# New planner costs and new order for a fused linear-attention and softmax-attention kernel

## The chip, the cores and the metric

One core of a Trainium2 chip. The metric is device time in microseconds of one execution, median over runs. The engines are TensorE (PE; its weight loads are PEld), VectorE (DVE), ScalarE (ACT), GpSimd (POOL) and SyncE (SP, whose queue issues most DMAs).

## The reference

Two attention blocks over 2048 tokens of width 512, 32 heads of 16, each with its own input and weights; their outputs are set side by side.

```python
# A: linear attention
phi = lambda t: jnp.where(t > 0, t + 1, jnp.exp(t)) + 1e-6
pq, pk = phi(q), phi(k)
kv = jnp.einsum("bhsd,bhse->bhde", pk, v)
z = jnp.einsum("bhsd->bhd", pk)
num = jnp.einsum("bhqd,bhde->bhqe", pq, kv)
den = jnp.einsum("bhqd,bhd->bhq", pq, z)[..., None] + 1e-6
o_a = num / den                      # then @ wo
# B: softmax attention
scores = jnp.einsum("bhqd,bhkd->bhqk", q, k) * Dh ** -0.5
p = softmax(scores)
o_b = jnp.einsum("bhqk,bhkd->bhqd", p, v)   # then @ wo
```

## The kernel before

Nearly all work is B's scores: 32 heads x 2048 x 2048. They are cut in 2048 blocks of 128 keys by 512 queries. A unit is four heads (row groups g of TensorE) with one chunk of 512 queries, 64 blocks; there are 32 units. Each block has one matmul for its scores (`qk`, L899) and is then exponentiated by one of two ways.

- **ScalarE's way.** The scores stand in the five PSUM banks `pS`; one ACTIVATE (L1111) reads two banks (1024 columns) or three (1536) and writes `PT` in f16. One output matmul for each block (L1306, PT with VV) adds it to `pPV`. Two slots of `pS` alternate, so that TensorE fills one while ScalarE reads the other.
- **VectorE's way.** The scores stand in one of two banks `pD`, or in the third bank of `pS` when ScalarE does not need it. One TENSOR_SCALAR (L1015) makes of them the integer whose bits are an f16 exponential, in `DI`. Two shifted copies of it follow, made from groups of up to two blocks (`DG`): most on GpSimd (L1226 for one group or several in one instruction, L1201 for a first and a second copy of two groups together), some on VectorE (L1170, and L1235 for the last unit alone). Three output matmuls take the three versions (one with the weights VX, two with VV), whose sum is a better exponential.

VectorE also evicts every projection (L595, L638, L647, L709, L764), normalises units (L1335, L1340, L1346), and does the second half of A's phi (L722, L724), whose exponential is ScalarE's EA (L721). A's jobs and the projections (`bjobs`, `ajobs`) are laid between the scores.

The order of the work is not written by hand. When the program is built, a planner keeps a clock `T` for each engine and again and again takes the piece of work that could start first; what it takes is added to its engine's queue. Engines then run their queues strictly in that order and wait on semaphores, so the planner's numbers set only the order. They are

- durations: an exponential is a fixed part + 0.000833 us a column (in `fill_act_cand`'s `run` and in `phi_stages`), a projection round `MM`, a round of output matmuls 0.218 us (`pv_cand`);
- delays between engines: `LTO` from the engine that writes to the one that reads, `LPE` from an engine's end until what it read can be filled again, `SWT` when TensorE changes the kind of matmul;
- the table `SEG`: one row of knobs for each 12 us of TensorE's planned time. `RW` is how early a score matmul may stand before ScalarE needs it, `RMX` and `DPR` how many blocks go to VectorE with it and how soon, `DBL` and `PBL` the backlog of VectorE and GpSimd above which no further block goes that way, `PVR`, `PVQ` and `PVO` how output matmuls are gathered, `DE2` and `DE3` from how few remaining blocks of the last unit on no block goes to VectorE and shifts of the last unit are VectorE's. `NZ` and `SD` add a noise, with its seed, to ties.

The last unit ends in `last_unit` (L1396 to L1401, two halves), four output projections (L1358) and four stores.

Of the kernel before, what the change touches and what calls it, by code (L numbers as in the profile page):

```python
# [238 lines left out]
def bass_concat_heads__linear_attn_block__softmax_full_mha__prompt_kernel(nc, A_x, A_wqkv, A_wo, B_x, B_wqkv, B_wo, out):  # L239
# [11 lines left out]
    JM = 2  # L251
    JX = 1
# [76 lines left out]
    )  # L329
    GB = 0.0  # L330
    PM = -0.025
    JN = 4
    KSL = 0.02
    PFX = 0.272
    FIDLE = 0.8
    AEND = 60.0
    RW = 0.3
    EQ = 20.0
    FPB = 4.0
# [28 lines left out]
    with es:  # L368
# [675 lines left out]
        def fill_act_cand():  # L1044
# [24 lines left out]
            def run(st, en):  # L1069
# [34 lines left out]
                if tk:  # L1104
                    d_emit(tk, T["pe"])
                w = 512 * len(bl)
                d = 0.052 + w * 0.000833
                exps.append(d)
                def ex(st_, en_):
                    exps.pop(0)  # L1110
# [626 lines left out]
```

## Time and profile before

| | |
|---|---|
| median of 3 runs | 661.06 us (660.82 to 661.22) |
| the profiled execution | 660.68 us, span 657.8 us |
| TensorE's granted clock | 1.000 |
| busy share PE, DVE, ACT, POOL | 97%, 97%, 98%, 90% |
| instructions of DVE, ACT, POOL | 1099, 696, 407 |

The span goes from the first to the last instruction; some 2.9 us of the execution's time lie around it. Busy time counts a record from its start to its end. Records of one engine can overlap, so two engines can both look full; how far apart records end tells more.

### The profile page before, as it was taken

To read this page: it belongs to the slowest core of one execution; us is meant where nothing else is said; L and a number is where in the kernel's file an instruction comes from. 1 tells how busy PE (TensorE), PEld (TensorE's weight loads), DVE (VectorE), ACT (ScalarE), POOL (GpSimd) and SP (SyncE) were. 2 spreads that over 40 slices of the span, in tenths; PEclk is the share of its full clock that TensorE was granted. 3 is DMA by queue.
4 is the path that set the end of the run, shared out by engine and by line. 5 is a ranking of instruction groups with operands and counts; after the bars stand their busy time and mean duration, and the time that the engine had idled before them with its cause. 6 is when DMAs were issued, how large, how long until landed. Compare 5 with 4: busy or idle time off the path is not lost.

```text
span 657.8 us, 19264 instructions
## 1 busy us (share of the span) xinstructions
PE 640.0 (97%) x8318; PEld 214.3 (33%) x8318; DVE 635.1 (97%) x1099; ACT 643.1 (98%) x696; POOL 589.9 (90%) x407
## 2 busy tenths in 40 slices
PE   8999999999999999999999999999999999999996
PEld 5333333232333333332232232322223322232222
DVE  4999999999999999999999999999999999999995
ACT  6999999999999999999999999999999999999995
POOL 5899999999999999999999999999999989999892
PEclk9999999999999999999999999999999999999999
DMA  9701010110101111002111011100110010011001
GB/s 185 202 1 33 3 34 2 33 26 10 34 2 34 34 34 35 1 17 74 26 33 42 1 34 34 26 11 8 23 25 13 2 33 26 9 34 49 22 29 46
DMA packets 53227, 21.75 MB, mean 33 GB/s; under 512 B 44176, under 2 KB 52624, under 8 KB 53136
## 3 DMA queue, kind: packets, MB, share of 16 engines
q1 hardware_dynamic: 51664, 19.80, 12.9%
q8 instruction: 67, 1.10, 0.7%
q10 hardware_dynamic: 1472, 0.66, 0.4%
q14 instruction: 24, 0.20, 0.1%
HBM read 4.46 MB, written 4.19 MB: 13 GB/s over the span
## 4 chain that ended last, share of the span: by engine, by line
ACT 84%; PE 11%; DVE 3%; DMA 1%; issue 0%; DVEq 0%
ACT PT L1111 82%; PE pPV L1306 4%; PE pS L899 3%; PE pD L609 2%; ACT EA L721 2%; DVE DI L1015 2%; DMA xTb<-in_B_x_dram 1%; DMA KNa<-VNa 1%; PE pD L899 1%; PE pS L609 0%; PE pD L1358 0%; DVE DI L1235 0%; PE pS L1442 0%; PE pS L1358 0%; DVE VNa L811 0%
## 5 line engine op out<-in xcount | busy, mean ns | idle before, releaser
L1111 ACT ACTIVATE PT<-pS 128x1024 f16<-128x1024 f32 (+1 forms) x658 | 630.7, 1151 | 1.7 <-PE pS L899 1.0
L1226 POOL TENSOR_SCALAR DI<-DI 128x2048 int16<-128x2048 int16 (+2 forms) x289 | 481.0, 1664 | 41.0 <-DVE DI L1015 22.9
L1015 DVE TENSOR_SCALAR DI<-pD 128x512 int16<-128x512 f32 x475 | 312.7, 679 | 6.0 <-PE pD L899 2.2
L899 PE MATMUL pS<-QT,KM 32*128 32x512 bf16 x1573 | 260.5, 384 | 7.4 <-ACT PT L1111 6.0
L1306 PE MATMUL pPV<-PT,VV 128*17 128x512 f16 x1361 | 235.3, 381 | 0.2 <-DVE OT L1335 0.2
L1306 PE MATMUL pPV<-DI,VV 128*17 128x512 f16 x1374 | 229.9, 382 | 0.3 <-POOL DI L1226 0.2
L899 PE MATMUL pD<-QT,KM 32*128 32x512 bf16 x475 | 171.2, 384 | 0.6 <-DVE DI L1015 0.6
L1306 PE MATMUL pPV<-DI,VX 128*17 128x512 f16 x687 | 160.5, 381 | 0.3 <-DVE OT L1335 0.2
L899 PEld LDWEIGHTS pS<-QT,KM 32*128 32x128 bf16 x1573 | 65.2, 91 | 243.2 <-ACT PT L1111 197.2
L1015 DVE TENSOR_SCALAR DI<-pS 128x512 int16<-128x512 f32 x212 | 143.8, 678 | 0.2 <-PE pS L899 0.2
L1170 DVE TENSOR_SCALAR DI<-DI 128x1056 int16<-128x1056 int16 x109 | 74.1, 687 | 0.5
L1201 POOL TENSOR_SCALAR DI<-DI 128x2048 int16<-128x2048 int16 x37 | 70.2, 1897 | 4.7 <-POOL DI L1226 1.6
L1306 PEld LDWEIGHTS pPV<-DI,VV 128*17 128x17 bf16 x1374 | 51.0, 88 | 46.9 <-issue 34.1
L1306 PEld LDWEIGHTS pPV<-PT,VV 128*17 128x17 bf16 x1361 | 52.4, 88 | 41.0 <-issue 31.3
L1306 PEld LDWEIGHTS pPV<-DI,VX 128*17 128x17 bf16 x687 | 36.4, 88 | 21.2 <-issue 15.4
L899 PEld LDWEIGHTS pD<-QT,KM 32*128 32x128 bf16 x475 | 40.6, 91 | 7.1 <-DVE DI L1015 3.6
L609 PE MATMUL pD<-xTb,Wb 128*32 128x512 bf16 x368 | 29.2, 384 | 0.6 <-DVE VV L709 0.5
L609 PE MATMUL pD<-Wa,xTa 128*32 128x256 bf16 x704 | 28.8, 275 | 0.1
L1335 DVE STREAM_TRANSPOSE OT<-pPV 128x512 f32<-128x512 f32 x31 | 21.9, 707 | 0.1
L1341 POOL TENSOR_TENSOR OT<-OT,ZR 128x256 bf16<-128x256 f32 x31 | 19.2, 620 | 3.0 <-DVE ZR L1340 1.4
L609 PE MATMUL pD<-Wa,KNa 128*32 128x512 bf16 x240 | 19.6, 384 | 0.8 <-DMA KNa<-VNa 0.7
L609 PEld LDWEIGHTS pD<-Wa,xTa 128*32 128x32 bf16 x704 | 15.2, 96 | 11.0 <-issue 6.6
(144 smaller groups left out, 381.1 us busy)
## 6 DMA issues: line engine op xcount, KB each, us to landing
out_dram<-KNa SPq DMA_DIRECT2D x31, 128.0 KB, 1.7
Wa<-in_A_wqkv_dram SPq DMA_DIRECT2D x1, 1536.0 KB, 8.6
KM<-KR SPq DMA_DIRECT2D x96, 16.0 KB, 1.8
Wb<-in_B_wqkv_dram SPq DMA_DIRECT2D x2, 384.0 KB, 4.1
Wb<-in_B_wqkv_dram SPq DMA_DIRECT2D x1, 512.0 KB, 4.7
Wa<-in_A_wo_dram SPq DMA_DIRECT2D x1, 512.0 KB, 5.5
Wa<-in_B_wo_dram SPq DMA_DIRECT2D x1, 512.0 KB, 3.7
ON<-in_B_x_dram ACTq DMA_DIRECT2D x1, 256.0 KB, 3.1
```

Of the source, the lines that this page charges most:

```text
L609: ins = self.e.matmul(out_[32 * g:32 * g + 32], lhsT=lhsT[:, 32 * g:32 * g + 32], rhs=rhs, start=start, stop=stop, tile_position=(0, 32 * g))
L721: ("act", 0.052 + n * 0.000833, f_ev("act", lambda e, bk: e.activation(EA[:, 0:n], f32v(bk)[:, c0:c0 + n], ACTF.Exp), [], ["EA"])),
L899: return e.matmul(dst, lhsT=KM[32 * g:32 * g + 32, Gp % 2, e_, j * 128:(j + 1) * 128], rhs=QT[32 * g:32 * g + 32, Gp % 2, c * 512:(c + 1) ...
L1015: sch.add("dve", lambda e: e.tensor_scalar(DI[:, di_at(0, buf) + i * 512:di_at(0, buf) + (i + n) * 512], f32v(DBANK[b0], n * 512), ESC, EB ...
L1111: sch.add("act", lambda e: e.activation(PTf[:, p0 * 512:p0 * 512 + w], S5[:, c0:c0 + w], ACTF.Exp, scale=SC), reads=skeys(sl, len(bl)), wr ...
L1170: sch.add("dve", lambda e: e.tensor_scalar(gapped(DI, di_at(v, buf), wide // 32, 32), DI[:, di_at(0, buf) - 32:di_at(0, buf) + w], 1.0, fl ...
L1201: sch.add("pool", lambda e: e.tensor_scalar(dv, sv, 1.0, float(SHIFT[0]), op0=ALU.mult, op1=ALU.add), reads=keys, writes=[("DI", v_, x) fo ...
L1226: sch.add("pool", lambda e: e.tensor_scalar(dv, sv, 1.0, sh_, op0=ALU.mult, op1=ALU.add), reads=keys, writes=[("DI", v, x) for x in best])
L1306: sch.add("pe", lambda e, g=g, j=j, c0=c0, V_=V_, r2=r2, P=P, first=first, last_=last_: e.matmul(PVb[32 * g:32 * g + 17, 0:512] if len(P.s ...
L1335: sch.add("dve", lambda e: e.transpose(OT[:, 0, :], PVb[:, 0:512]), reads=[("PV", g) for g in range(4)], writes=[("OT", 0)])
L1341: ("pool", 0.69, f_op("pool", lambda e: e.tensor_tensor(xn[:, :, 16 * e_:16 * e_ + 16], o[:, :, 0:16], zr.unsqueeze(2).broadcast_to([128, ...
```

## The change

It changes numbers of the planner, and so the order on every engine; no instruction's kind is new. The fixed part of an exponential rises from 0.052 to 0.0635 us and now stands for the distance between the ends of two ACTIVATEs in a row; the delay from TensorE to VectorE rises from 0.2 to 0.243; smaller corrections go with them. All 54 rows of `SEG` are new. Each has two more knobs that were constants before: `PTW`, by which two evictions from pD may become one, and `JN`, how many groups one shift may take. No pair of evictions is joined in the order that results.

```diff
     SEG = (
-        (0.0,0.1,4,3.0,6,1,6,4,9.0,26,3.0,7.0,0.8,0.8,2,7.0,2.0,2.5,0.5,2,1,0.3,4,10,0,0),
...
+        (0.0,0.2,4,0.8,6,1,8,2,10.0,28,2.5,6.0,0.5,2.5,2,4.0,2.0,2.5,0.5,2,1,0.1,8,0,-9.0,4,2,6),
...
-        LPE = {"dve": 0.136, "act": 0.176, "pool": PM, "pe": 0.2, "dma": 0.12}
-        LTO = {("pe", "dve"): 0.2, ("pe", "act"): 0.215, ("act", "dve"): 0.155, ("dve", "pool"): 0.163, ("pool", "dve"): 0.07, ("dve", "act"): 0.15}
-        SWT = 0.106
+        LPE = {"dve": 0.139, "act": 0.16, "pool": PM, "pe": 0.243, "dma": 0.12}
+        LTO = {("pe", "dve"): 0.243, ("pe", "act"): 0.215, ("act", "dve"): 0.137, ("dve", "pool"): 0.166, ("pool", "dve"): -0.03, ("dve", "act"): 0.15}
+        SWT = 0.107
...
-        MM = 0.218
+        MM = 0.224
...
-                ("act", 0.052 + n * 0.000833, f_ev("act", lambda e, bk: e.activation(EA[:, 0:n], f32v(bk)[:, c0:c0 + n], ACTF.Exp), [], ["EA"])),
+                ("act", 0.0635 + n * 0.000833, f_ev("act", lambda e, bk: e.activation(EA[:, 0:n], f32v(bk)[:, c0:c0 + n], ACTF.Exp), [], ["EA"])),
...
-                waiting[bi] = (buf, b, push("dve", en + 0.2, 0, 0.598, p1))
+                waiting[bi] = (buf, b, push("dve", en + LTO["pe", "dve"], 0, 0.598, p1))
...
-                d = 0.052 + w * 0.000833
+                d = 0.0635 + w * 0.000833
...
-            dur = 0.218 * bb[1]
+            dur = 0.2185 * bb[1]
...
-                        ptb[src[1]] = en + LPE["pe"]
+                        ptb[src[1]] = en + 0.2
...
-                        last_unit(u, en + 0.2)
+                        last_unit(u, en + 0.243)
                     else:
-                        push("dve", en + 0.2, -1, 0.63, lambda st_, en_: unit_done(u, en_))
+                        push("dve", en + 0.243, -1, 0.63, lambda st_, en_: unit_done(u, en_))
...
-                (_, RW, RMX, DPR, PTA, PTD, DNEXT, PVR, PVQ, PVO, DBL, PBL, DLEAD, AJP, FNR, FPB, FDB, PSH, DSH, JM, JX, PMW, DE2, DE3, NZ, SD) = seg.pop(0)
+                (_, RW, RMX, DPR, PTA, PTD, DNEXT, PVR, PVQ, PVO, DBL, PBL, DLEAD, AJP, FNR, FPB, FDB, PSH, DSH, JM, JX, PMW, DE2, DE3, PTW, JN, NZ, SD) = seg.pop(0)
```

What each engine has to do, before and now: ScalarE 613 exponentials of 1024 columns and 45 of 1536, now 613 and 43, with 32 EA in both; VectorE 687 L1015 and now 693 (475 from pD, now 505), 109 L1170 and now 111, six L1235 and now none; GpSimd 326 shift instructions and now 337; TensorE 3422 output matmuls and now 3434.

VectorE in the middle of the run, from the normalisation of the 20th unit on, before:

```order
L1335 STREAM_TRANSPOSE OT<-pPV 128x512
L1015 TENSOR_SCALAR DI<-pS 128x512
L1015 TENSOR_SCALAR DI<-pD 128x512
L709 CAST VV<-pD 128x32x16
L1015 TENSOR_SCALAR DI<-pD 128x512
L1340 RECIPROCAL ZR<-OT 128x16
L1170 TENSOR_SCALAR DI<-DI 128x33x32
L1015 TENSOR_SCALAR DI<-pD 128x512
L595 CAST KNa<-pD 128x512
L1015 TENSOR_SCALAR DI<-pS 128x512
L1346 STREAM_TRANSPOSE ON<-OT 128x512
```

and now:

```order
L1335 STREAM_TRANSPOSE OT<-pPV 128x512
L1015 TENSOR_SCALAR DI<-pD 128x512
L1340 RECIPROCAL ZR<-OT 128x16
L709 CAST VV<-pD 128x32x16
L1015 TENSOR_SCALAR DI<-pD 128x512
L1170 TENSOR_SCALAR DI<-DI 128x33x32
L1346 STREAM_TRANSPOSE ON<-OT 128x512
L1015 TENSOR_SCALAR DI<-pD 128x512
L1015 TENSOR_SCALAR DI<-pS 128x512
L1015 TENSOR_SCALAR DI<-pD 128x512 x2
L1015 TENSOR_SCALAR DI<-pS 128x512
```

The same kinds of rows stand there, in another order: the normalisation's steps come sooner and the evictions of blocks stand closer together behind them.

VectorE at the end, from the last blocks that it takes to the last unit's transposition (L1396), before:

```order
L1015 TENSOR_SCALAR DI<-pD 128x512 x3
L1235 TENSOR_SCALAR DI<-DI 128x1024 x2
L1015 TENSOR_SCALAR DI<-pD 128x512 x2
L1235 TENSOR_SCALAR DI<-DI 128x1024 x2
L1015 TENSOR_SCALAR DI<-pD 128x512
L1235 TENSOR_SCALAR DI<-DI 128x512 x2
L1396 STREAM_TRANSPOSE OT<-pPV 128x256
```

and now:

```order
L1015 TENSOR_SCALAR DI<-pD 128x512 x3
L1170 TENSOR_SCALAR DI<-DI 128x33x32
L1015 TENSOR_SCALAR DI<-pD 128x512 x4
L1170 TENSOR_SCALAR DI<-DI 128x33x32
L1015 TENSOR_SCALAR DI<-pD 128x512
L1396 STREAM_TRANSPOSE OT<-pPV 128x256
```

The six shifts of the last groups left VectorE; two stand there as L1170, the others went to GpSimd.

GpSimd at the end, from the normalisation of the last unit but one (L1341) to the three small products of the range flag (L695 to L697), before:

```order
L1341 TENSOR_TENSOR OT<-OT,ZR 128x16x16
L1226 TENSOR_SCALAR DI<-DI 128x1024 x2
L1226 TENSOR_SCALAR DI<-DI 128x2x1024
L1226 TENSOR_SCALAR DI<-DI 128x2048
L1201 TENSOR_SCALAR DI<-DI 128x2x1024
L1226 TENSOR_SCALAR DI<-DI 128x1024 x2
L695 TENSOR_TENSOR TP<-TP 1x1
```

and now:

```order
L1341 TENSOR_TENSOR OT<-OT,ZR 128x16x16
L1226 TENSOR_SCALAR DI<-DI 128x1024
L1226 TENSOR_SCALAR DI<-DI 128x2x1024
L1226 TENSOR_SCALAR DI<-DI 128x2048
L1226 TENSOR_SCALAR DI<-DI 128x1024
L1201 TENSOR_SCALAR DI<-DI 128x2x1024
L1226 TENSOR_SCALAR DI<-DI 128x1024
L1201 TENSOR_SCALAR DI<-DI 128x2x1024
L1226 TENSOR_SCALAR DI<-DI 128x512 x2
L695 TENSOR_TENSOR TP<-TP 1x1
```

Nine shift instructions stand there instead of seven, and the last two are of a single block.

106 rows, old and new, of the table SEG are left out of this document.

## Prediction

> **What bounds the kernel now.** I read the page's busy shares and chain first, then a table by stage, then ScalarE in order of time.
>
> ```profile
> span 657.8 us, 19264 instructions
> ...
> PE 640.0 (97%) x8318; PEld 214.3 (33%) x8318; DVE 635.1 (97%) x1099; ACT 643.1 (98%) x696; POOL 589.9 (90%) x407
> ...
> ACT 84%; PE 11%; DVE 3%; DMA 1%; issue 0%; DVEq 0%
> ...
> L1111 ACT ACTIVATE PT<-pS 128x1024 f16<-128x1024 f32 (+1 forms) x658 | 630.7, 1151 | 1.7 <-PE pS L899 1.0
> L1226 POOL TENSOR_SCALAR DI<-DI 128x2048 int16<-128x2048 int16 (+2 forms) x289 | 481.0, 1664 | 41.0 <-DVE DI L1015 22.9
> ```
>
> ```profile
> 0.00:50.00 50.00, 46.28 (x588) 20.36 (x588) 40.74 (x75) 43.79 (x47) 38.55 (x49) 1.00 0.56 127
> ...
> 450.00:500.00 50.00, 49.48 (x620) 14.80 (x613) 49.50 (x87) 50.00 (x57) 46.43 (x29) 1.00 0.08 20
> ...
> 600.00:650.00 50.00, 49.03 (x586) 13.63 (x583) 46.30 (x79) 48.74 (x48) 41.03 (x31) 1.00 0.09 28
> ```
>
> The columns of the table are PE, PEld, DVE, ACT and POOL busy time. Every engine is near full, and the chain that ended last lies 84% on ScalarE. A busy share cannot separate the engines here, because 658 exponentials of mean 1151 ns would be 757 us: records overlap. What an instruction really takes from ScalarE is the distance between its end and the end before it:
>
> ```profile
> 8.57 34.39 ACT L1111 ACTIVATE PT<-pS 128x1536 f16<-128x1536 f32 x35 [1.05 <-PE pS L899]
> 42.83 0.62 ACT L721 ACTIVATE EA<-pS 128x512 bf16<-128x512 f32 x1
> 43.31 12.48 ACT L1111 ACTIVATE PT<-pS 128x1024 f16<-128x1024 f32 x13
> 55.48 0.81 ACT L721 ACTIVATE EA<-pD 128x512 bf16<-128x512 f32 x1
> 55.96 4.91 ACT L1111 ACTIVATE PT<-pS 128x1024 f16<-128x1024 f32 x5
> ...
> 592.53 48.45 ACT L1111 ACTIVATE PT<-pS 128x1024 f16<-128x1024 f32 x49 [0.53 <-PE pD L899]
> ```
>
> The five of 55.96 end at 60.87, 4.58 us after the EA row's end at 56.29: 0.916 us each. The thirteen of 43.31 hold one of 1536 columns: from 43.45 to 55.79 are 12.34 us, less 12 x 0.916 leaves 1.35 us for the wide one. The EA row at 55.48 ends 0.50 us after them. The old planner reckons 0.905 for 1024 columns and 1.332 for 1536, the new one 0.9165 and 1.343, which is what these rows show.
>
> ```profile
> L1111 ACT ACTIVATE PT<-pS 128x1024 f16<-128x1024 f32 x613 | 578.3, 1123 | 0.6 <-PE pD L899 0.5
> ...
> L1111 ACT ACTIVATE PT<-pS 128x1536 f16<-128x1536 f32 x45 | 69.5, 1543 | 1.0 <-PE pS L899 1.0
> ```
>
> Over all: 613 x 0.917 + 45 x 1.343 + 32 EA x 0.49 = 638.3 us of ScalarE's work. The first exponential starts at 8.57, the last ends at 648.74 (635.00 + 13.74, a row shown at the tail): 640.2 us. So ScalarE stands still for some 2 us in the middle, the longest at 592.53 (0.53 us by its row), and it is the bound. Ahead of it lies a start of 8.6 us, behind it a tail of 9.1.
>
> VectorE is the next. Its records overlap too; a block's eviction (L1015) starts 0.60 us after the one before it if nothing is late:
>
> ```profile
> 455.33 0.68 DVE L1015 TENSOR_SCALAR DI<-pD 128x512 int16<-128x512 f32 x1
> 455.93 0.68 DVE L1015 TENSOR_SCALAR DI<-pS 128x512 int16<-128x512 f32 x1
> 456.73 0.69 DVE L1015 TENSOR_SCALAR DI<-pD 128x512 int16<-128x512 f32 x1
> 457.34 0.70 DVE L1346 STREAM_TRANSPOSE ON<-OT 128x512 bf16<-128x512 bf16 x1
> 457.96 0.65 DVE L1015 TENSOR_SCALAR DI<-pS 128x512 int16<-128x512 f32 x1
> 458.54 0.41 DVE L722 TENSOR_SCALAR EC<-EA 128x528 bf16<-128x528 bf16 x1
> 458.98 0.69 DVE L724 SCALAR_TENSOR_TENSOR PQT<-pD,EC 128x512 bf16<-128x512 f32 x1
> ```
>
> From 455.33 to 455.93 is 0.60, but from 455.93 to 456.73 is 0.80: a block from pD came 0.2 us late. Such losses are under the view's limit for a wait, so 49.50 of 50 us look busy.
>
> **The change part by part.** Both kernels compute the same 2048 score blocks; the order says which engine takes each.
>
> *ScalarE's work.* The order holds 613 exponentials of 1024 columns and 32 EA as before, and 43 of 1536 instead of 45. Two times 1.343 is 2.69 us less on the engine that bounds: -2.69. Bounds: the same two priced at the record's whole 1543 ns would be -3.09, and zero if ScalarE is no longer the bound.
>
> *VectorE's work.* It gets those six blocks: 693 L1015 instead of 687, +3.6 us at 0.60; two more L1170, +1.2 at 0.61 (as 457.34 to 457.96 for a like form); and six L1235 fewer, all in the tail:
>
> ```profile
> 643.58 1.50 DVE L1235 TENSOR_SCALAR DI<-DI 128x1024 int16<-128x1024 int16 x2
> 645.00 1.28 DVE L1015 TENSOR_SCALAR DI<-pD 128x512 int16<-128x512 f32 x2
> 646.31 0.76 DVE L1235 TENSOR_SCALAR DI<-DI 128x1024 int16<-128x1024 int16 x2
> ...
> 647.71 0.49 DVE L1235 TENSOR_SCALAR DI<-DI 128x512 int16<-128x512 int16 x2
> ```
>
> They hold VectorE for 1.42 + 0.68 + 0.49 = 2.6 us at a place where it has 3.7 us to spare in 50 (46.30 busy). The +4.8 us come in the body, where it has little.
>
> How little is the term that decides. I put these prices (0.60 for L1015 and casts, 0.61 for L1170, 0.62 for transposes, 0.335 for L722, 0.66 for L724) on every VectorE row of both orders and compared with ScalarE's work up to the same block. In the old order VectorE's work falls 6.3 us behind ScalarE's between ScalarE's 25th and 475th us; in the new one only 1.2 us, and from the 250th to the 475th it falls behind by 0.5. So VectorE could lose 6.3 us there and not hold up ScalarE; now it may lose 1.2. In the profile of before it lost 7.2 us there (the 6.3 and ScalarE's own 0.9 us of stalls in that stretch). Lower bound of its loss in the new order: what no order from TensorE changes, VectorE instructions that follow one they depend on (L724 starts 0.44 after L722 instead of 0.335; some L1170 behind the L1015 that they read), together some 2.5 us. Then ScalarE stalls 1.3 us instead of 0.9: +0.4. Upper bound: it loses the 7.2 again, ScalarE stalls 6.0: +5.1. I take a loss of 3.3, a stall of 2.1, +1.2, near the lower end: the larger part of the losses is like the row at 456.73, a block from TensorE that came late, and the new planner counts TensorE to VectorE 43 ns longer (0.243 for 0.2), which puts those matmuls earlier. Behind a late eviction stand the other VectorE rows, and TensorE's next pD matmul, which waits for the bank and has ScalarE's next scores queued behind it.
>
> *TensorE.* Six more blocks as DI cost three output matmuls instead of one, +12, in rounds of four. Rounds follow at 0.22 us (300.47, 300.69 below): 3 rounds, +0.7 us over the whole run, less 8 filler matmuls. Beside ScalarE, so nothing; if TensorE has no room it is at most +0.7.
>
> ```profile
> 300.47 0.39 PE L1306 MATMUL pPV<-DI,VV 128*17 128x512 f16 x3
> ...
> 300.69 0.38 PE L1306 MATMUL pPV<-PT,VV 128*17 128x512 f16 x2
> ```
>
> *GpSimd.* Ten more shifts of 1024, one of 2048 fewer, two of 512 new: 10 x 1.12 - 1.98 + 2 x 0.70 = +10.6 us, from the two rows below (2.17 for two; 1.90 and a gap of 0.07) and, for 512, half of the column time less. It waited 22.9 us for L1015 (page), so this is covered in the body; half of that cover is spent.
>
> *The tail.* Of the 10.6 some 4.6 us replace L1235 at the end.
>
> ```profile
> 635.00 13.74 ACT L1111 ACTIVATE PT<-pS 128x1536 f16<-128x1536 f32 x12
> ...
> 640.33 1.90 POOL L1201 TENSOR_SCALAR DI<-DI 128x2048 int16<-128x2048 int16 x1 [0.15 <-POOL DI L1226]
> ...
> 642.30 2.17 POOL L1226 TENSOR_SCALAR DI<-DI 128x1024 int16<-128x1024 int16 x2
> ...
> 650.55 0.40 POOL L1398 TENSOR_TENSOR OT<-OT,ZR 128x128 bf16<-128x128 f32 x1 [5.16 <-DVE ZR L1397]
> ```
>
> GpSimd's last shift ended at 644.47, 4.3 us ahead of the last exponential's end at 648.74. With 4.6 us more it ends about with it. The last blocks for VectorE stand ahead of three exponentials instead of two, 0.9 us earlier. I take 0; bounds -0.2 (three output-projection matmuls now stand ahead of the last output matmuls) to +1.3 (the two shifts of 512 entirely behind the last exponential).
>
> *The start.* TensorE and ScalarE begin alike up to the first exponential; its 8.6 us stay. SP's queue keeps its 191 rows, with the K copies (L652) and stores (L841) a few places from where they stood; its transfers take little of the span, so 0.
>
> Where the change lengthens a shift, a rule on ports speaks against it. The rows first:
>
> ```profile
> L1201 POOL TENSOR_SCALAR DI<-DI x37: 1897/1897/1899, 53.5 to 640.3; 128x2048 int16<-128x2048 int16 x37
> ...
> L1235 DVE TENSOR_SCALAR DI<-DI x6: 285/414/1174, 643.6 to 647.9; 128x1024 int16<-128x1024 int16 x4, 128x512 int16<-128x512 int16 x2
> ```
>
> Minimum, median and maximum in ns: GpSimd's 37 shifts never varied though VectorE worked beside them all the time; only one L1235, the first, took 1174 for 414, while GpSimd shifted. The Trainium skill, "SBUF — State Buffer", section "Who interferes with whom", says that a VectorE tensor_scalar in a two-port mode and any GpSimd instruction shut each other out for a whole instruction. By that rule each of the two added L1170 could cost 1.9 us behind a shift, +3.8, and the sum would be 663.0; the trace agrees for L1235, which the new order no longer has, and not for L1170, beside which no shift grew.
>
> **Sum.** 660.68 (the profiled execution's own time, span 657.8 and 2.9 around it) - 2.69 + 1.2 + 0 = 659.2. That execution lay 0.38 under the median of the three runs, 661.06, which is 0.06%; I leave the sum as it is.
>
> **The rivals.** A measurement of this kernel can tell about 0.2%, 1.3 us, from no change: faster is below 659.7, slower above 662.4.
>
> *VectorE eats the gain (same).* It loses 4.8 to 7 us in ScalarE's 25th to 475th us, ScalarE stalls 3.6 to 5.8 instead of 0.9: 660.68 - 2.69 + 2.7 to 4.9 is 660.7 to 662.9, mostly within 0.2%. For it: a stretch of 225 us that must run at 99.8% of VectorE's best pace, where 98.4% was seen (7.2 lost in 450). Against it: these losses happened while ScalarE held up TensorE, so part was spare time.
>
> *VectorE becomes the bound (slower).* The old plan reckoned each of ScalarE's 690 instructions 0.0115 us too short, which left every other engine 7.9 us of room in the run; the new plan takes this room away. If VectorE and TensorE, still reckoned without some of their real delays, lose 2% of it over the whole body, as the 0.65 us lost in the 19.4 us from 454.74 on would be three in a hundred, then ScalarE stalls 7 us or more: 660.68 - 2.69 + 5 to 8 = 663 to 666. It decides from a stall of 4.4 us beyond the 2 of before. Against it: from the 475th us on the new order again leaves VectorE some 7 us.
>
> ```profile
> 454.74 0.68 DVE L638 CAST QT<-pD 128x512 bf16<-128x512 f32 x1
> ...
> 474.18 0.65 DVE L1015 TENSOR_SCALAR DI<-pS 128x512 int16<-128x512 f32 x1
> ```
>
> *GpSimd's tail (same).* The two shifts of 512 come last and the final output matmuls wait: +1.3, 660.5.
>
> *GpSimd and VectorE stop each other (slower).* If the two added L1170 each wait for a whole shift as the first L1235 did, 1.9 us by the L1201 row, 659.2 + 3.8 = 663.0. Against it: the 109 L1170 of before stretched none of the 37 shifts of that row. This is the case of the "SBUF — State Buffer" page of the Trainium skill.
>
> *All stalls go.* The better prices also remove the 2 us: 660.68 - 2.69 - 2 = 656.0.
>
> **How the numbers follow.** Forecast (ScalarE stays the bound, stalls of 2 to 4 us, 657.2 to 659.7): 0.40. All stalls go (656 to 657.2): 0.10. VectorE eats the gain: 0.23; GpSimd's tail: 0.05. VectorE becomes the bound: 0.20; GpSimd and VectorE stop each other: 0.02. So faster 0.50, same 0.28, slower 0.22. The range leaves 0.1 out on each side: from 656.4, in the case without stalls, to 663.6, inside the slow case; the forecast's own range is 657.2 to 659.7.
>
> **What would show it.** ScalarE's records: 613, 43 and 32, at 0.917, 1.343 and 0.49 us between ends, span near 656.3. Right: idle time ahead of L1111 stays near 2 us and no window of the body shows ScalarE under 49.8 of 50. Wrong by VectorE: in the windows from 250 to 475 ScalarE falls to 49.5 or less with PE pS as its releaser, VectorE without idle time. Wrong in the tail: GpSimd's last L1226 ends after the last exponential, and the last output matmul more than 0.9 us behind it. The prediction falls if ScalarE's stalls pass 4 us, wherever they lie.

## The result, and the profile after

| | before | after |
|---|---|---|
| median, runs on the same chip | 661.16 us (660.82 to 661.25) | 657.67 us (657.45 to 658.05) |
| the profiled execution, its span | 660.68, 657.8 us | 657.45, 655.7 us |
| first exponential's start to the last one's end | 640.17 us | 637.95 us |
| of that ScalarE's work / stalls | 638.2 / 1.9 us | 635.5 / 2.4 us |

The ratio of after to before is 0.9949 (0.9934 to 0.9963): 3.4 us faster. The forecast was 659.2, range 656.4 to 663.6; the sum was 1.7 us too high against the profiled execution.

The page of the kernel after: the span, the busy shares, the chain of work that ended last, and the groups.

```profile
span 655.7 us, 19281 instructions
...
PE 639.1 (97%) x8321; PEld 215.3 (33%) x8322; DVE 633.4 (97%) x1101; ACT 641.4 (98%) x694; POOL 600.2 (92%) x418
...
DVE 45%; PE 32%; ACT 17%; POOL 3%; DMA 1%; issue 1%; DVEq 0%; POOLq 0%
...
L1111 ACT ACTIVATE PT<-pS 128x1024 f16<-128x1024 f32 (+1 forms) x656 | 627.2, 1101 | 1.2 <-PE pS L899 1.0
L1226 POOL TENSOR_SCALAR DI<-DI 128x2048 int16<-128x2048 int16 (+2 forms) x300 | 491.6, 1639 | 33.7 <-DVE DI L1015 13.3
L1015 DVE TENSOR_SCALAR DI<-pD 128x512 int16<-128x512 f32 x505 | 330.6, 678 | 4.0 <-PE pD L899 2.4
```

The busy shares say nearly the same as before. The chain does not: ScalarE's share of it falls from 84% to 17%, VectorE has 45% and TensorE 32%. The wait of GpSimd for L1015, its cover in the prediction, fell from 22.9 to 13.3 us.

The table by stage (PE, PEld, DVE, ACT, POOL) hardly shows it. ScalarE misses 0.06 us in 50, VectorE is fuller, and its slack of the end (43.86 of 50) is larger:

```profile
250.00:300.00 50.00, 49.35 (x611) 16.47 (x607) 49.82 (x89) 49.94 (x55) 47.03 (x33) 1.00 0.16 39
...
450.00:500.00 50.00, 49.59 (x619) 15.11 (x617) 49.70 (x87) 50.00 (x54) 47.48 (x31) 1.00 0.07 18
...
600.00:650.00 50.00, 49.01 (x566) 14.12 (x567) 43.86 (x77) 47.23 (x48) 43.80 (x36) 1.00 0.09 26
```

The groups by shape show it better, in the length of ScalarE's records:

```profile
L1111 ACT ACTIVATE PT<-pS 128x1024 f16<-128x1024 f32 x613 | 574.8, 1073 | 0.2
L1111 ACT ACTIVATE PT<-pS 128x1536 f16<-128x1536 f32 x43 | 64.2, 1494 | 1.0 <-PE pS L899 1.0
```

The same 613 instructions have a mean of 1073 ns instead of 1123, and yet most ends still lie 0.917 us apart. A record runs from its start, which may lie inside the one before, to its end. So a short record (the shortest take 1017 ns) is one that started late inside the one before. The share of records under 1050 ns rose from 17% to 37%, which I read as scores that come later, shortly before they are needed, without yet being late. The experiments below agree: the share is 8% in e3, where ScalarE hardly ever waits, and 56% in l6, where VectorE is given more work. So this column is a gauge of how near the bound is to changing hands, where idle time shows 0.2 us.

VectorE where it ran with gaps before, now from 253.56 on, in order of time:

```profile
253.56 0.68 DVE L1015 TENSOR_SCALAR DI<-pS 128x512 int16<-128x512 f32 x1
254.16 1.27 DVE L1015 TENSOR_SCALAR DI<-pD 128x512 int16<-128x512 f32 x2
255.35 0.67 DVE L1015 TENSOR_SCALAR DI<-pS 128x512 int16<-128x512 f32 x1
255.95 0.68 DVE L1015 TENSOR_SCALAR DI<-pD 128x512 int16<-128x512 f32 x1
```

Five starts in a row 0.60 us apart, none late. Between 35 and 485 us the evictions L1015 that ended more than 50 ns late were 39 before, 4.9 us in all, and are 23 now, 2.4 us.

The tail, in order of time on GpSimd, PEld, VectorE and ScalarE:

```profile
645.08 1.32 POOL L1226 TENSOR_SCALAR DI<-DI 128x512 int16<-128x512 int16 x2
```

```profile
646.45 0.09 PEld L1306 LDWEIGHTS pPV<-DI,VV 128*17 128x17 bf16 x1 [0.58 <-POOL DI L1226]
```

```profile
647.10 0.45 DVE L1396 STREAM_TRANSPOSE OT<-pPV 128x256 f32<-128x256 f32 x1 [3.22 <-PE pPV L1306]
```

```profile
638.50 8.01 ACT L1111 ACTIVATE PT<-pS 128x1536 f16<-128x1536 f32 x7
649.23 0.60 ACT L595 ACTIVATE KNa<-pD 128x512 bf16<-128x512 f32 x1 [2.72 <-PE pD L1358]
```

GpSimd's last shift ends at 646.40 and the last exponential at 646.50, together, as forecast. A weight load of TensorE waits 0.58 us for the shift, but beside that exponential.

### The profile page after: what moved, and what is told of

The parts are those of the page before. It is cut to its first block, busy times and chain, and to the rows that moved or that the text cites. A ratio compares the mean times of both kernels' runs of the same rounds, so it can differ in the third digit from the quotient of the medians.

```text
span 655.7 us, 19281 instructions
## 1 busy us (share of the span) xinstructions
PE 639.1 (97%) x8321; PEld 215.3 (33%) x8322; DVE 633.4 (97%) x1101; ACT 641.4 (98%) x694; POOL 600.2 (92%) x418
## 3 DMA queue, kind: packets, MB, share of 16 engines
q1 hardware_dynamic: 51664, 19.80, 13.2%
## 4 chain that ended last, share of the span: by engine, by line
DVE 45%; PE 32%; ACT 17%; POOL 3%; DMA 1%; issue 1%; DVEq 0%; POOLq 0%
DVE DI L1015 30%; ACT PT L1111 17%; PE pPV L1306 11%; PE pS L899 11%; PE pD L609 6%; DVE DI L1170 5%; POOL DI L1226 2%; PE pS L609 2%; DVE OT L1335 1%; DVE KNa L724 1%; DVE VNa L764 1%; DVE VV L709 1%; DVE EC L722 1%; POOL DI L1201 1%; DMA xTb<-in_B_x_dram 1%
## 5 line engine op out<-in xcount | busy, mean ns | idle before, releaser
L1226 POOL TENSOR_SCALAR DI<-DI 128x2048 int16<-128x2048 int16 (+2 forms) x300 | 491.6, 1639 | 33.7 <-DVE DI L1015 13.3
L1015 DVE TENSOR_SCALAR DI<-pD 128x512 int16<-128x512 f32 x505 | 330.6, 678 | 4.0 <-PE pD L899 2.4
L899 PE MATMUL pD<-QT,KM 32*128 32x512 bf16 x505 | 181.2, 384 | 0.1
L1306 PE MATMUL pPV<-DI,VX 128*17 128x512 f16 x693 | 162.7, 381 | 0.7 <-DVE OT L1335 0.7
L1015 DVE TENSOR_SCALAR DI<-pS 128x512 int16<-128x512 f32 x188 | 127.5, 678 | 0.1
L1170 DVE TENSOR_SCALAR DI<-DI 128x1056 int16<-128x1056 int16 x111 | 75.8, 690 | 0.3
L1201 POOL TENSOR_SCALAR DI<-DI 128x2048 int16<-128x2048 int16 x37 | 70.3, 1900 | 4.5 <-POOL DI L1226 1.8
L899 PEld LDWEIGHTS pD<-QT,KM 32*128 32x128 bf16 x505 | 43.4, 91 | 6.6 <-DVE DI L1015 4.6
L609 PE MATMUL pD<-Wa,xTa 128*32 128x256 bf16 x608 | 24.2, 275 | 0.3 <-DVE DI L1015 0.3
L609 PE MATMUL pD<-xTb,Wb 128*32 128x512 bf16 x304 | 23.9, 384 | 0.1
L1341 POOL TENSOR_TENSOR OT<-OT,ZR 128x256 bf16<-128x256 f32 x31 | 19.3, 622 | 1.8
L609 PE MATMUL pS<-Wa,xTa 128*32 128x256 bf16 x416 | 16.9, 275 | 0.4 <-DVE DI L1015 0.4
L609 PEld LDWEIGHTS pD<-Wa,xTa 128*32 128x32 bf16 x608 | 13.2, 96 | 9.0 <-issue 5.3
```

The costliest lines, as they stand in the source:

```text
L609: ins = self.e.matmul(out_[32 * g:32 * g + 32], lhsT=lhsT[:, 32 * g:32 * g + 32], rhs=rhs, start=start, stop=stop, tile_position=(0, 32 * g))
L899: return e.matmul(dst, lhsT=KM[32 * g:32 * g + 32, Gp % 2, e_, j * 128:(j + 1) * 128], rhs=QT[32 * g:32 * g + 32, Gp % 2, c * 512:(c + 1) ...
L1015: sch.add("dve", lambda e: e.tensor_scalar(DI[:, di_at(0, buf) + i * 512:di_at(0, buf) + (i + n) * 512], f32v(DBANK[b0], n * 512), ESC, EB ...
L1170: sch.add("dve", lambda e: e.tensor_scalar(gapped(DI, di_at(v, buf), wide // 32, 32), DI[:, di_at(0, buf) - 32:di_at(0, buf) + w], 1.0, fl ...
L1201: sch.add("pool", lambda e: e.tensor_scalar(dv, sv, 1.0, float(SHIFT[0]), op0=ALU.mult, op1=ALU.add), reads=keys, writes=[("DI", v_, x) fo ...
L1226: sch.add("pool", lambda e: e.tensor_scalar(dv, sv, 1.0, sh_, op0=ALU.mult, op1=ALU.add), reads=keys, writes=[("DI", v, x) for x in best])
```

## The experiments

All ScalarE figures are worked out as in the prediction: work = count by 0.917, 1.343 and 0.49; stalls = first exponential's start to last one's end, less the work. They are those of the profiled execution, in us. Each kernel ran beside the kernel before on the same chip, whose median there lay between 660.4 and 661.2 us; so kernels of different rows are compared by their ratios and not by their medians.

| | us, median | ratio to before | exps 1024 / 1536 | work | stalls |
|---|---|---|---|---|---|
| before | 661.16 | 1 | 613 / 45 | 638.2 | 1.9 |
| after | 657.67 | 0.9949 (0.9934 to 0.9963) | 613 / 43 | 635.5 | 2.4 |
| e1 new costs, old table | 666.72 | 1.0096 (1.0080 to 1.0111) | 604 / 55 | 643.4 | 2.9 |
| e2 old costs, new table | 669.67 | 1.0135 (1.0119 to 1.0150) | 595 / 62 | 644.6 | 5.4 |
| e3 after, old price of an exponential | 663.67 | 1.0050 (1.0037 to 1.0064) | 604 / 56 | 644.8 | 0.3 |
| e4 after, old TensorE-to-VectorE delay | 665.42 | 1.0074 (1.0060 to 1.0087) | 612 / 46 | 638.7 | 4.8 |
| l5 before + VectorE work | 661.73 | 1.0015 (1.0006 to 1.0024) | 613 / 45 | 638.2 | 3.1 |
| l6 after + VectorE work | 660.92 | 1.0003 (0.9994 to 1.0012) | 613 / 43 | 635.5 | 5.5 |
| r1 after - VectorE work | 657.21 | 0.9953 (0.9939 to 0.9966) | 613 / 43 | 635.5 | 2.0 |
| r2 before - VectorE work | 660.79 | 1.0002 (0.9993 to 1.0011) | 613 / 45 | 638.2 | 2.2 |

### Parts of the change

`e1_costs_only` keeps every new cost and puts the old 54 rows back (with the two new knobs at their former constants):

```diff
-        (0.0,0.2,4,0.8,6,1,8,2,10.0,28,2.5,6.0,0.5,2.5,2,4.0,2.0,2.5,0.5,2,1,0.1,8,0,-9.0,4,2,6),
+        (0.0,0.1,4,3.0,6,1,6,4,9.0,26,3.0,7.0,0.8,0.8,2,7.0,2.0,2.5,0.5,2,1,0.3,4,10,-9.0,4,0,0),
...
```

> The new costs with the old table of knobs (PTW -9.0 and JN 4, as the constants were). Its order holds 604 exponentials of 1024 columns and 55 of 1536: 643.4 us of ScalarE's work, 5.2 more than before. If ScalarE's work sets the time and the costs alone are worth nothing without a table fitted to them: 661.1 + 5.2 = 666.3, 665 to 669 with stalls. If the truer prices by themselves make the order better: below 661, with ScalarE's work wrong as a measure.

`e2_table_only` is the kernel before with the new 54 rows.

> The new table with the old costs. 595 and 62 exponentials: 644.6 us of ScalarE's work, 6.4 more than before. By ScalarE's work: 667.5, 666 to 669, with few stalls, since the old costs leave the other engines room. If the table carries the gain whatever the costs: 658 to 660.

Neither half is faster. With the costs alone the planner hands ScalarE 10 more wide exponentials, for 9 narrow ones fewer: work +5.2 us on before, stalls +1.0, and the time follows (+6.3 by the ratio). That is what was expected. With the table alone work is +6.4, and stalls add 3.5, some 2 us more time than expected. Of its 5.4 us of stalls 3.3 stand before one exponential, at 47.5 us, after TensorE's granted clock (the third number from the end) had fallen:

```profile
37.00:38.00 1.00, 0.63 (x4) 0.09 (x2) 1.00 (x3) 1.00 (x2) 0.69 (x2) 1.00 0.00 0
38.00:39.00 1.00, 0.55 (x2) 0.10 (x2) 0.97 (x2) 1.00 (x2) 1.00 (x1) 0.55 0.00 0
39.00:40.00 1.00, 0.66 (x5) 0.10 (x3) 0.33 (x1) 1.00 (x2) 0.94 (x2) 0.50 0.00 0
...
47.00:48.00 1.00, 1.00 (x9) 0.12 (x8) 0.55 (x2) 0.52 (x1) 0.92 (x2) 0.50 0.00 0
48.00:49.00 1.00, 1.00 (x20) 0.34 (x12) 0.36 (x2) 1.00 (x2) 1.00 (x2) 0.83 0.02 8
```

The times of e2's four runs follow their mean granted clock: 670.53 us at 0.990 (the profiled one), 669.86 at 0.993, 669.47 and 669.05 at 0.996. So part of what e2 lost goes with this fall.

The gain belongs to the pair, table and costs, and not to the better costs or to a better table.

`e3_old_exp_price` and `e4_old_pe_dve` put one cost of the changed kernel back, under the new table:

```diff
-                d = 0.0635 + w * 0.000833
+                d = 0.052 + w * 0.000833
```

> The changed kernel with the exponential's fixed part back at 0.052 us, all else new. 604 and 56 exponentials: 644.8 us of ScalarE's work, 9.3 more than the changed kernel. By ScalarE's work: 657.7 + 9.3 = 667, less up to 1 us of its stalls. If ScalarE's price does not matter: 658.

```diff
-        LTO = {("pe", "dve"): 0.243, ...
+        LTO = {("pe", "dve"): 0.2, ...
...
-                        last_unit(u, en + 0.243)
+                        last_unit(u, en + 0.2)
```

> The changed kernel with the delay from TensorE to VectorE back at 0.2 us, all else new. 612 and 46 exponentials: 638.7 us of ScalarE's work, 3.2 more than the changed kernel: 660.9 by that alone. If the short delay also brings VectorE's late blocks back (7 us lost in 450 instead of 3), ScalarE stalls 2 to 4 us more: 662 to 665. If neither counts: 658.

In e3 ScalarE, reckoned cheaper, gets 9.3 us more work than in the changed kernel and stalls only 0.3 us in all, the least of any run: it is the bound alone, and the chain says so. By the ratios e3 is 6.7 us slower than the changed kernel, where 8.3 to 9.3 was expected: 2.1 us of stalls went. In e4 the work is +3.2 and the stalls +2.4 on the changed kernel. By the ratios it is 8.3 us slower, more than the 4.3 to 7.3 that was expected; its tail is the rest: the last eviction ends 5.8 us behind the last exponential instead of 4.2, and the end of the execution comes 0.9 us later behind that. The first row is e3's chain; the group rows are L1015 from pD in before, e3 and e4:

```profile
ACT 92%; DVE 4%; PE 3%; DMA 1%; issue 0%; DVEq 0%
```

```profile
L1015 DVE TENSOR_SCALAR DI<-pD 128x512 int16<-128x512 f32 x475 | 312.7, 679 | 6.0 <-PE pD L899 2.2 <-PE pS L899 1.9
```

```profile
L1015 DVE TENSOR_SCALAR DI<-pD 128x512 int16<-128x512 f32 x467 | 308.3, 678 | 13.2 <-PE pD L899 8.5 <-PE pS L899 3.2
```

```profile
L1015 DVE TENSOR_SCALAR DI<-pD 128x512 int16<-128x512 f32 x481 | 315.9, 677 | 11.3 <-PE pD L899 5.9 <-PE pS L899 4.2
```

VectorE's idle time ahead of L1015 doubles in both against before and triples against the 4.0 of after, waiting for TensorE. In e4 that is the term the longer delay was to remove, but e3 has it with the long delay, and e1 and e2 have more still (15.6 and 16.3). Every one of these four kernels has an order of its own from start to end, so what they show is the price of another order and only in part the price of the number that was put back.

### VectorE's room, with the order held

To test the disputed term the order must not move. The next kernels add instructions, or shorten them, where the planner does not reckon them, so that every engine's queue stays as it was.

In l1 and l2 it is a small write of VectorE:

```diff
+        def extra(lane, every, fn, reads=()):
+            xn["n"] += 1
+            if xn["n"] % every == 0:
...
+                sch.add(lane, lambda e: fn(e, XS[:, i:i + 1]), reads=reads)
...
+                    extra("dve", 9, lambda e, x: e.memset(x, 0.0))
```

> The kernel before with one small VectorE write (a MEMSET of one column nobody reads) behind every ninth L1015, 76 in all, unknown to the planner, so that every other instruction keeps its place; by its cost, measured here, some 4 to 6 us more work for VectorE. If ScalarE alone bounds the old order and VectorE has 6 us of room: +0 to +2 us. If VectorE has no room in either order: +4 or more.

> The same 77 writes in the changed kernel (same rule). If the new order has used up VectorE's room, most of the 4 to 6 us appears: +3 to +5, and ScalarE's stalls grow by as much. If ScalarE is still the only bound: +0 to +2, as in the old order.

```profile
L1027 DVE MEMSET XS<- x76: 59/59/59, 24.9 to 643.7; 128x1 bf16 x76
```

l1 took 660.71 us (ratio 1.0001, 0.9992 to 1.0010) and l2 657.99 (0.9959, 0.9946 to 0.9973). The records are there, 59 ns each, but the ends of the two L1015 around one stayed 597 to 598 ns apart (median), as without it. The load was none, and both runs say nothing on VectorE's room; they show how much two executions of one order differ.

The same was done in the changed kernel for ScalarE (l3, behind every 40th exponential an ACTIVATE of one column) and for GpSimd (l4, behind every 8th shift a MEMSET):

```diff
+                    extra("act", 40, lambda e, x: e.activation(x, identf[:, 0:1], ACTF.Exp), ["identf"])
```

> The changed kernel with one ACTIVATE of one column behind every 40th exponential, 16 in all, unknown to the planner; some 0.2 us each, 3 us in all. If ScalarE is the bound everywhere: +3. If ScalarE and VectorE share the bound by turns: +1 to +2, since part falls where ScalarE would have waited for VectorE.

```diff
+                    extra("pool", 8, lambda e, x: e.memset(x, 0.0))
```

> The changed kernel with one small GpSimd write behind every eighth shift of L1226's kind, some 37, unknown to the planner; 0.1 to 0.3 us each, 4 to 10 us of GpSimd. If GpSimd's 16 us of waits are room: +0 to +1. If the eleven added shifts have made it a bound beside the others: most of it, +3 or more.

l3 took 657.72 us (0.9960, 0.9946 to 0.9974) and l4 657.76 (0.9954, 0.9940 to 0.9968). On ScalarE one took 82 to 96 ns between ends, 1.4 us for 16. The way from the first exponential to the last grew by 1.6, from 637.95 to 639.57 us, but not all of that is the load: 1.0 us of it are two stalls at 16 and 17 us, ahead of the first added instruction (48.3 us). l4 has the same two with 1.1 us. There TensorE's projection waits for a transfer of x that came in time in the profile of after. First l3, then after:

```profile
13.49 0.39 PE L908 MATMUL pS<-QT,KM 32*128 32x512 bf16 x2
14.79 0.83 PE L618 MATMUL pD<-xTb,Wb 128*32 128x512 bf16 x12 [0.91 <-DMA xTb<-in_B_x_dram]
```

```profile
13.64 0.39 PE L899 MATMUL pS<-QT,KM 32*128 32x512 bf16 x2
13.96 0.83 PE L609 MATMUL pD<-xTb,Wb 128*32 128x512 bf16 x12
```

Behind that, from ScalarE's 25th us of work on, the way grew by 0.65 us, half of the 1.4: the rest fell where ScalarE would have stalled. That is what was expected if ScalarE shares the bound, in kind; the size rests on one execution, and the time of all runs, +0.7 us by the ratios, can't tell it from the whole. No such load was run in the old order. GpSimd's 37 cost some 30 ns net each, 1.1 us, too little to tell anything; l4's way grew by 1.0 us, all in those first two stalls.

Then comes a load that is one, a TENSOR_SCALAR behind every 20th L1015, in the old order (l5) and in the new (l6):

```diff
+                    extra("dve", 20, lambda e, x: e.tensor_scalar(gapped(XS, 0, 5, 21), identf[:, 0:105], 1.0, 0.0, op0=ALU.mult, op1=ALU.add), ["identf"])
```

> The kernel before with a small TENSOR_SCALAR of VectorE (128x105, SBUF to SBUF) behind every 20th reshape L1015, and nothing else. What one costs is read as the growth of the distance between the ends of the L1015s on both sides of it; estimate 0.15 to 0.2 us each, 5 to 6 us in all. If VectorE has room of its own in the old order (6.3 us in ScalarE's 25th to 475th us of work, which lost 7.2), the old order takes nearly all of it without a change of time: 0 to +2 us. If ScalarE's stalls follow VectorE's work one for one, +5 to +6.

> The changed kernel with the same small TENSOR_SCALARs. If VectorE's room in the new order is used up (1.2 us of room, 3.1 lost with the stalls), most of the added work comes out as ScalarE stalls: +3 to +6 us over the changed kernel. If ScalarE's own work alone still sets the body, 0 to +1, as in the old order.

One moves the ends of the L1015 around it from 598 to 767 ns, 0.169 us; 34 are 5.7 us, of which 24 (old order) and 25 (new) lie in ScalarE's 25th to 475th us of work, 4.1 and 4.2 us. ScalarE's stalls in that stretch (those over 20 ns) grew from 0.6 to 1.1 us in the old order and from 1.9 to 4.4 in the new. The way from the first to the last exponential grew by 1.1 and 3.1 us, the time by 1.0 and 3.6 by the ratios. The chains of l5 and l6:

```profile
ACT 38%; PE 34%; DVE 24%; DMA 2%; SPq 1%; issue 0%; DVEq 0%
```

```profile
DVE 66%; PE 25%; ACT 5%; POOL 2%; issue 1%; DMA 1%; ACTq 0%; DVEq 0%; POOLq 0%
```

and a stretch of the new order with the load, where ScalarE (fourth) now misses time and VectorE (third) is the fullest:

```profile
300.00:350.00 50.00, 49.47 (x616) 14.72 (x612) 49.90 (x90) 49.92 (x55) 47.14 (x30) 1.00 0.13 31
350.00:400.00 50.00, 48.62 (x577) 15.24 (x573) 49.88 (x90) 49.88 (x57) 46.81 (x26) 1.00 0.12 25
```

So the order of the two rooms is shown as the prediction had it: the old order takes seven eighths of VectorE's added work without a stall, the new order two fifths. Their sizes, 6.3 and 1.2 us, are not shown.

The last pair goes the other way. Every 30th L1015 works on 256 columns instead of 512, 23 in the new order (r1) and 22 in the old (r2); the second halves of those blocks are left out:

```diff
+                    xn[0] += 1
+                    wd = 256 if xn[0] % 30 == 0 else n * 512
...
-DI[..., i * 512:... + (i + n) * 512], f32v(DBANK[b0], n * 512),
+DI[..., i * 512:... + i * 512 + wd], f32v(DBANK[b0], n * 512)[:, 0:wd],
```

> The changed kernel with every 30th L1015 reading and writing 256 columns instead of 512, 23 in all, in the same order: it leaves out the second half of those 23 blocks. By the row of the small TENSOR_SCALAR (0.169 us for 105 columns) and 0.598 for 512, one takes about 0.33, so VectorE has some 6 us less to do. If VectorE's lack of room causes the stalls that are left (1.9 us in ScalarE's 25th to 475th us), they fall to 0.7 or less and the kernel gains 1 to 2 us on the changed one, and ScalarE's share of the chain rises again. If the stalls come from TensorE's own order, 0 to -0.4.

> The kernel before with the same 23 evictions halved. VectorE's room is not used up there and ScalarE stalls only 0.6 us in that stretch: 0 to -0.5 us by both. A gain like that of the changed kernel would say that VectorE held the old order too.

A halved eviction ends 0.33 us behind the one before it instead of 0.60, as expected; 17 of them, 4.6 us, lie in ScalarE's 25th to 475th us of work. r2 is at the time of before. In r1 the gain of 1 to 2 us did not come: it is no different from the changed kernel by the ratios (0.9953 for 0.9949), and the stalls in the stretch fell from 1.9 to 1.5, not to 0.7. The fall is larger than what executions of this order without relief differ by: l2 has 2.05 there and l4 1.8. Exponential by exponential over the whole body, the changed kernel has 35 stalls over 20 ns, 2.45 us. With VectorE relieved 28 of them stand before the same exponentials with 2.00 of their 2.09 us, the seven others (0.37 us) are gone, and no new one came. With VectorE loaded (l6) all 35 are there, 0.95 us longer, and 29 new ones of 2.1 us. The chain of r1 is

```profile
PE 45%; ACT 40%; DVE 12%; POOL 2%; DMA 1%; issue 1%; ACTq 0%; DVEq 0%; POOLq 0%
```

VectorE's share of the chain fell from 45% to 12%, though hardly any stall went with it: the chain names who stood on the way, not what that work costs.

Take one of the two largest of the 28: ScalarE's exponential at 253.15 of the changed kernel ends 1.088 us after the one before it instead of 0.917. TensorE ahead of it:

```profile
251.63 0.39 PE L899 MATMUL pS<-QT,KM 32*128 32x512 bf16 x2
251.95 0.84 PE L609 MATMUL pD<-Wa,xTa 128*32 128x256 bf16 x24
252.72 0.39 PE L899 MATMUL pS<-QT,KM 32*128 32x512 bf16 x3
```

and the same place in r1, where VectorE had time:

```profile
251.46 0.39 PE L900 MATMUL pS<-QT,KM 32*128 32x512 bf16 x2
251.78 0.84 PE L610 MATMUL pD<-Wa,xTa 128*32 128x256 bf16 x24
252.55 0.39 PE L900 MATMUL pS<-QT,KM 32*128 32x512 bf16 x3
```

Both times 1.09 us lie between two fills of pS, because 24 projection matmuls stand between them; no engine holds TensorE up there, and ScalarE empties a pair of banks in 0.917. The 28 are not all so clear. In r1's trace no wait for VectorE lies between the last two fills ahead of 18 of them (1.2 of the 2.0 us); ahead of the other ten one does, in nine only of a weight load, which runs beside TensorE's matmuls. In the stretch from the 25th to the 475th us it is 16 places with 1.1 us and six with 0.3.

## Why the prediction was right or wrong

| step | forecast | profiled execution |
|---|---|---|
| ScalarE's work | -2.69 | -2.69 (613, 43 and 32 records) |
| ScalarE's stalls in its 25th to 475th us | +1.2 (0.9 to 2.1) | +1.3 (0.6 to 1.9) |
| ScalarE's other stalls | 0 | -0.8 |
| start | 0 | 0.0 (8.57 and 8.56; 8.3 to 9.1 in other executions of the two orders) |
| last exponential to the last store's issue | 0 (-0.2 to +1.3) | -0.6 |
| behind that | 0 | -0.4 |
| sum | -1.5 | -3.2 |

- **ScalarE's work** was right, count and price (the sum is 638.2 us, not 638.3). That ScalarE is no longer alone as the bound is shown by l6, where 3.1 of 5.7 us of VectorE's added work came out, against 1.1 in l5; l3 points the same way. That it was the bound before rests on its chain, 84%, and on l5: no work was added to ScalarE in the old order.
- **VectorE's room** was right as a comparison of the two orders: 4 us more work cost 0.5 us of stalls in the old order and 2.5 in the new.
- **VectorE's loss as the cause of the stalls** was wrong, though its number came out (2.1 forecast, 1.9 measured). The loss of 3.3 us taken for VectorE comes out at 3.1 (1.2 of room and 1.9 of stalls), but that sum holds whoever causes the stalls, so the agreement was luck and proves nothing. Under relief 0.4 us of the 1.9 go, and 1.5 stay at the same places of the order. The step that failed is the sentence on TensorE, "beside ScalarE, so nothing": it priced TensorE's work over the whole run, where what counts is how much of it stands between two fills of pS. Of the 1.5, 1.1 are TensorE's own by r1's trace, where no wait for VectorE lies between the fills; whose the other 0.3 are stays open, since a late eviction there could hold TensorE up and six microseconds of relief, spread over the run, need not reach it.
- **The rivals "VectorE eats the gain" and "VectorE becomes the bound"** did not come about; l6 is what the first looks like.
- **The one large stall of before**, 0.53 us at 592.53, is not in the new order. The forecast counted it among what stays; it is the larger part of the -0.5 behind the 475th us. Another -0.4 lies in the first 25 us and is a matter of one transfer, the x that TensorE waits for in the rows of l3. In the four profiled executions of the old order it landed at 14.4 to 15.0 us and cost 0.3 to 0.6 us of stalls; in the new order it landed at 12.3 to 13.2 us in four and cost nothing, and at 14.7 and 14.9 in two (l3 and l4) and cost 1.0 and 1.1. The step of the forecast that failed there is "its transfers take little of the span, so 0". Nor does the new order assure the early landing, so this 0.4 is in part luck of the execution compared. These -0.8 are the largest thing that the sum missed.
- **The tail** was mis-sized, outside its bounds. L1396's first half starts 0.60 us after the last exponential's end instead of 1.04 (647.10 less 646.50): one round of output matmuls was left behind it. Another 0.1 is the step from L1401 to ScalarE's L595 (0.93 us for 1.06), for which the projections that now stand ahead were rightly named. The last eviction ended 4.81 us behind the last exponential in all four profiled executions of the old order and 4.1 to 4.2 in all six of the new. GpSimd's shifts did end with the last exponential, and it cost nothing: the rival of its tail did not come about.
- **Behind the last store** 0.4 us stay open. From the last eviction to the end of the execution it took 6.8 to 7.4 us in the four executions of the old order and 5.7 to 6.9 in the six of the new; nothing in the order there differs, and nothing was tried on it.
- **GpSimd and VectorE shutting each other out** was not seen with two more L1170: the 37 L1201 have 1900 ns throughout and the 111 L1170 at most 703.

```profile
L1170 DVE TENSOR_SCALAR DI<-DI x111: 642/693/703, 26.2 to 642.6; 128x1056 int16<-128x1056 int16 x111
```

```profile
L1201 POOL TENSOR_SCALAR DI<-DI x37: 1900/1900/1902, 49.3 to 643.1; 128x2048 int16<-128x2048 int16 x37
```

By the rule of the Trainium skill ("SBUF — State Buffer", section "Who interferes with whom") some of these records would have grown by a whole partner's instruction if L1170 ran in a two-port mode. None did; whether it runs in such a mode, no run here tells.

## What to carry to other kernels

Where a planner sets the order, putting one of its costs back changes the whole order, and the run then prices an order and not a cost; add or take away a known load that the planner does not see, in both orders, and compare stall by stall. When two engines have equal work, a shortage of one and the stalls of the other add up by arithmetic, so a number that agrees does not name a cause; only a run that relieves the suspect does. Once ScalarE's work has been cut to what the others can follow, look for stretches between two fills of its banks that are longer than it needs to empty them (here 1.09 for 0.917 us). And before a small difference is laid to an order, look at another execution of the same order: here one transfer that landed 2 us later moved the body by 1 us.

## What the runs showed of the hardware

- A VectorE MEMSET of one column, 59 ns by its record, took nothing from its queue between two evictions; a TENSOR_SCALAR of 105 columns with a record of 0.25 us took 0.169; an ACTIVATE of one column with a record of 0.25 us took 0.084 (median). The record is not the price here; the growth of the distance between ends is.
- An exponential's ends lie 0.917 us apart for 1024 columns and 1.343 for 1536, so 64 ns and 0.832 ns a column, while the shortest record is 1017 ns. The Trainium skill ("Perfetto Trace Analysis", section "Optimizing Scalar/DVE Operations") gives some 51 ns of overhead for ScalarE on PSUM and says that a profiled instruction shows about twice its overhead because the last part overlaps with the next; the overlap agrees, and the fixed part was 64 here.
- TensorE's granted clock fell to 0.50 for ten microseconds in e2, in the rows above, after a microsecond with four matmuls in it, and came back after full ones. The Trainium skill ("TensorE: Matmul & The Clock Gate", Part 1) has the clock fall to half after an idle window of about 3.4 us. Half agrees; but TensorE was not idle ahead of it: by its records, whose ends are modelled, it was 0.91, 0.83 and 0.63 busy in the three microseconds before, with 10, 7 and 4 matmuls. So a thin stretch was enough here. No other profile here fell to it in the body. ScalarE's stall of 3.3 us lies inside those ten microseconds; that the clock made it is argued, not shown.
- A transfer of x, issued 6.4 to 7.1 us into the span, took 5.9 to 6.5 us to land in four of ten executions and 7.8 to 8.0 in the other six.
